# Making phi(q) of the first part for four head pairs at once, and one denominator for two score tiles

## The chip, the cores and the metric

The kernel runs on one core of a Trainium2 chip. Its time is the device time of one execution, in microseconds; smaller is better. The engines that matter here are PE (TensorE, the matmuls), ACT (ScalarE), DVE (VectorE), POOL (GpSimd) and SP, which issues the DMAs. They run side by side and wait for each other through semaphores.

## The reference, cut to what matters

An attention layer with a memory term feeds two feed-forward layers. B, H, S, D = 4, 8, 576, 64; 2304 tokens, width 512, hidden width 2048.

```python
scores = scale * q @ k.T, causal;  a = exp(scores - max)
a /= a.sum(-1) + 1e-09             # the denominator
local = a @ v
q_p = phi(q)                       # phi(x) = where(x > 0, x, exp(x) - 1) + 1
mem_out = (q_p @ M_prev) / (q_p @ z_prev + 1e-06)
g = 1 / (1 + exp(-beta))           # per head
attn = g * mem_out + (1 - g) * local
x = moe(attn)                      # x @ w_in, relu squared, s * . + b, @ w_out
out = moe2(x)                      # x @ w_in, a clipped square, @ w_out
```

## The kernel before, in words

The eight heads of a batch are four **head pairs** (two heads of 64 fill 128 partitions). The queries are cut into eight **parts**: for each of four batches first the tokens 0 to 255 (group `lo`, tiles 1 and 0), later the tokens 256 to 575 (group `hi`). The first two parts are computed ahead of everything; after them the blocks of the first feed-forward layer follow, with the other parts between them.

Nothing in the program is ordered by hand. Each operation is given to a planner (`Plan`, L108) with its engine, or several engines to choose from, and a cost; the planner lays out one order for each engine, and fixes on which engine an elementwise operation runs. So an edit at one place can move instructions at many others. Where the planner sees PE without work in the first phase it puts in idle matmuls on a tile of zeros (`zr`, L1379); they compute nothing that is used.

For one head pair of a `lo` part the work is:

- `att_front` (L769), **phi**: `qn + 1` on POOL (L801), exp(qn) on ACT (L522, the helper's line), min and max of both on DVE (L804), times z on DVE or POOL (L806, L805), a sum for each head on DVE (L807), two small DVE operations that make 1 / ((sum + 1e-6)(1 + exp(-beta))) (L808, L811), and phi times that on POOL or DVE (L812, L813). PE transposes the result (L820), and a copy takes it out of PSUM.
- `att_scores` (L830): PE makes the scores of tiles 1 and 0 (L861, eight matmuls). DVE adds the mask and takes the minimum of the negated scores (L877: 256 columns of tile 1 and 128 of tile 0 for each head). ACT takes exp with its sum (L522). DVE makes the **denominator** of each tile, `(sum + 1e-9) * (1 + exp(beta))`, in two small operations (L891, L894), and ACT, POOL or DVE multiplies the array by it (L903, L901, L902).
- `att_flip` (L907, transposes at L921, copies at L537 or L538) and `att_sum` (L928, matmuls at L937 and L948): transposes, then memory term and a @ v in one PSUM bank, whose result is split into a high and a low half for the feed-forward layer (`xx`, L537 and L529).

`constants` (L565) makes 1 + exp(beta) and 1 + exp(-beta) from the row that is loaded with z, and four DVE operations of 64 partitions (L573, L575) turn the first into the two orders that a joint tile of two heads needs.

In the same early time the weights of the first layer come in by DMA as 32 chunks of 64-bit words, and each is **converted** by two elementwise operations on ACT or POOL (L596 or L598, L602 or L600) and two on DVE (L605, L607), then split in two halves (L537 or L542, L529 or L533). The feed-forward matmuls of the first layer are L1008 to L1010 and L1071 to L1076.

In the trace the tiles of the first two parts lie in buffers that later hold weights, and have their names: `wor8` to `wor11` (phi, its helper, its transposed copy, q) and `wir12` to `wor15` (the score arrays).

Of the kernel before, what the change touches and what calls it, by code (L numbers as in the profile page):

```python
# [373 lines left out]
def tile_kernel(ctx: ExitStack, tc: tile.TileContext, qk_in, nv_in, z_in, w_in, w_out, w2_in, w2_out, out):  # L374
# [190 lines left out]
    def constants(zb):  # L565

        def row(a, e):
            return zb.t[:, H * D + a:H * D + e]
        act(lambda: con[:, 16:24], lambda: row(0, 8), AF.Exp, 8, [zb], ["con"], ATT)
        act(lambda: con[:, 24:32], lambda: row(0, 8), AF.Exp, 8, [zb], ["con"], ATT, scale=-1.0)  # L570
        dve(0.08, lambda: nc.vector.tensor_scalar(con[:, 16:32], con[:, 16:32], 1.0, None, ALU.add), ["con"], ["con"], ATT)
        for j in range(2):
            dve(0.08, lambda rows=slice(64 * j, 64 * j + 64), j=j: nc.vector.tensor_scalar(  # L573
                con[rows, 32:36], con[rows, 16:24].rearrange("p (n two) -> p n two", two=2)[:, :, j], 1.0, None, ALU.mult), ["con"], ["con"], ATT)
            dve(0.08, lambda rows=slice(64 * j, 64 * j + 64), j=j: nc.vector.tensor_scalar(  # L575
                con[rows, 36:40], con[rows, 16:24].rearrange("p (n two) -> p n two", two=2)[:, :, 1 - j], 1.0, None, ALU.mult), ["con"], ["con"], ATT)
        dve(0.08, lambda: nc.vector.tensor_scalar(con[:, 0:2], row(8, 10), 1.0, None, ALU.mult), [zb], ["sb"], W1)
        dve(0.05, lambda: nc.vector.memset(con[:, 4:5], 0.5), [], ["sb"], W1)
        dve(0.05, lambda: nc.vector.memset(con[:, 5:6], 1.0), [], ["sb"], W1)
# [186 lines left out]
    def load_z(b, zb):  # L766
        dma(lambda: zb.t, lambda: z_in[b], P * (H * D + 16) * 4, [], [zb], LOAD if first_qk[2:] else ATT, [zb], None if first_qk[2:] else "first")

    def att_front(hp, g, qn, q_key, zb):  # L769

        nt, nq = len(GROUPS[g]), GLEN[g]
        t0, n2 = min(GROUPS[g]), nt * P
        ee, xt, pg = (x.take() for x in ((E_EE, E_UZ, E_PG) if early_part[0] else (R_EE, R_UZ, R_PG)))
        cf = R_CF.take()
        hs = slice(hp * P, hp * P + P)

        def e():
            return ee.t[:, 0:n2]

        def pz():  # L780
            return xt.t[:, 0:n2]

        def c():
            return cf.t[:, 0:2 * nt]

        def cells(x):
            return x.t[:, 0:n2].rearrange("p (t d) -> p t d", d=D)
# [4 lines left out]
        def zz():
            return zb.t[:, hs].unsqueeze(1).broadcast_to([P, nt, P])

        def cc():
            return c().unsqueeze(2).broadcast_to([P, 2 * nt, D])

        def c2():
            return c().rearrange("p (t h) -> p t h", h=2)

        add([("POOL", c_pool(n2), lambda: nc.gpsimd.tensor_scalar(pz(), qn(), 1.0, 1.0, ALU.add, ALU.mult)),  # L801
             ("DVE", c_dve(n2, "cp"), lambda: nc.vector.tensor_scalar(pz(), qn(), 1.0, None, ALU.add))], [q_key], [xt], ATT, [xt])
        act(e, qn, AF.Exp, n2, [q_key], [ee], ATT, acq=[ee])
        dve(c_dve(n2), lambda: nc.vector.scalar_tensor_tensor(e(), e(), 1.0, pz(), ALU.min, ALU.max), [xt], [ee], ATT)  # L804
        add([("POOL", c_pool(n2, "tt"), lambda: nc.gpsimd.tensor_tensor(tiles3(xt), tiles3(ee), zz(), ALU.mult)),  # L805
             ("DVE", c_dve(n2), lambda: nc.vector.tensor_tensor(tiles3(xt), tiles3(ee), zz(), ALU.mult))], [ee, zb], [xt], ATT)  # L806
        dve(c_dve(n2), alone(lambda: nc.vector.tensor_reduce(c(), cells(xt), AX.X, ALU.add)), [xt], [cf], ATT, [cf])  # L807
        dve(0.08, lambda: nc.vector.scalar_tensor_tensor(  # L808
            c2(), c2(), 1e-6, con[:, 24 + 2 * hp:26 + 2 * hp].unsqueeze(1).broadcast_to([P, nt, 2]), ALU.add, ALU.mult),
            ["con"], [cf], ATT)  # L810
        dve(0.09, alone(lambda: nc.vector.reciprocal(c(), c())), [], [cf], ATT)  # L811
        add([("POOL", c_pool(n2, "tt") - 0.13, lambda: nc.gpsimd.tensor_tensor(cells(ee), cells(ee), cc(), ALU.mult)),  # L812
             ("DVE", c_dve(n2), lambda: nc.vector.tensor_tensor(cells(ee), cells(ee), cc(), ALU.mult))], [cf], [ee], ATT)  # L813
# [16 lines left out]
    def att_scores(g, items, mems=()):  # L830
# [38 lines left out]
        for hp, qk, t, c0, c1, places in items:  # L869
# [3 lines left out]
            pi = 0 if c0 == 0 else 1  # L873

            m0 = 0 if c1 < w else 640 if t == 4 else 512 - t * P + c0
            for j, (a, (x, at)) in enumerate(zip(arrays, places)):
                dve(c_dve(c1 - c0) + 0.02, alone(lambda a=a, s=s, z=zs[x], c0=c0, c1=c1, m0=m0, pi=pi, j=j, at=at, ao=ao: nc.vector.tensor_tensor_reduce(  # L877
                    a.t[:, ao + c0:ao + c1], z.t[:, at:at + c1 - c0], mask[:, m0:m0 + c1 - c0], -SCALE,
                    BIG if pi == 0 else s.t[:, j:j + 1], ALU.add, ALU.min, s.t[:, 2 * pi + j:2 * pi + j + 1])),
                    [zs[x], "mask", "zero_aa", (a, "new"), (s, "new")], [(a, hp, t), (s, "min", j)], ATT)  # L880
            if c1 < w:
                continue
            for j, a in enumerate(arrays):
                def view(w=w, a=a, ao=ao):
                    return a.t[:, ao:ao + w]

                act(view, view, AF.Exp, w, [(s, "min", j)], [(a, hp, t), (s, "sum", j)],
                    ATT, ap=2, bias=lambda s=s, x=2 * pi + j: s.t[:, x:x + 1], scale=-1.0,
                    accum_out=lambda s=s, x=4 + j: s.t[:, x:x + 1])
            c = 32 + hp + 4 * turned(hp, t) if t == 4 else 16 + 2 * hp  # L890
            dve(0.13, lambda s=s, nh=nh, c=c: nc.vector.scalar_tensor_tensor(  # L891
                s.t[:, 6:6 + nh], s.t[:, 4:4 + nh], 1e-9, con[:, c:c + nh], ALU.add, ALU.mult),
                [(s, "sum", j) for j in range(nh)] + ["con"], [(s, "r")], ATT)
            dve(0.08, alone(lambda s=s, nh=nh: nc.vector.reciprocal(s.t[:, 8:8 + nh], s.t[:, 6:6 + nh])), [(s, "r")], [(s, "i")], ATT)  # L894
            for j, a in enumerate(arrays):
                def view(w=w, a=a, ao=ao):
                    return a.t[:, ao:ao + w]

                def col(s=s, j=j):
                    return s.t[:, 8 + j:9 + j]  # L900
                add([("POOL", c_pool(w) + 0.09, lambda view=view, col=col: nc.gpsimd.tensor_scalar(view(), view(), col(), 1.0, ALU.mult, ALU.mult)),  # L901
                     ("DVE", c_dve(w, "cp") + 0.06, lambda view=view, col=col: nc.vector.tensor_scalar(view(), view(), col(), None, ALU.mult)),  # L902
                     ("ACT", c_act(w, 1), lambda view=view, col=col: nc.scalar.activation(view(), view(), AF.Copy, scale=col()))],  # L903
                    [(s, "i")], [(a, hp, t)], ATT)
# [554 lines left out]
```

## Time and profile before

| | us |
|---|---|
| median of 3 runs (973.88 to 974.11) | 973.88 |
| the profiled execution | 974.04 |
| its span, first to last instruction | 972.2 |
| PE busy | 963.5 (99%) |
| DVE busy | 660.0 (68%) |
| ACT busy | 582.0 (60%) |
| POOL busy | 225.4 (23%) |

The span is 1.84 us shorter than the profiled execution's own time. The granted TensorE clock is at full speed in every slice. The shares are means over stages: busy shares of the first 100 us are far from these. PE's busy time also holds the idle matmuls, so a busy PE is not always a PE that does needed work.

### The profile page before, as it was taken

To read this page: it belongs to the slowest core of one execution; us is meant where nothing else is said; L and a number is where in the kernel's file an instruction comes from. 1 tells how busy PE (TensorE), PEld (TensorE's weight loads), DVE (VectorE), ACT (ScalarE), POOL (GpSimd) and SP (SyncE) were. 2 spreads that over 40 slices of the span, in tenths; PEclk is the share of its full clock that TensorE was granted. 3 is DMA by queue.
4 is the path that set the end of the run, shared out by engine and by line. 5 is a ranking of instruction groups with operands and counts; after the bars stand their busy time and mean duration, and the time that the engine had idled before them with its cause. 6 is when DMAs were issued, how large, how long until landed. Compare 5 with 4: busy or idle time off the path is not lost.

```text
span 972.2 us, 19818 instructions
## 1 busy us (share of the span) xinstructions
PE 963.5 (99%) x7548; PEld 870.8 (90%) x7548; DVE 660.0 (68%) x1548; ACT 582.0 (60%) x1340; POOL 225.4 (23%) x339
## 2 busy tenths in 40 slices
PE   9999999999999999999999999999999999999998
PEld 7799999999999989999998888989998899998897
DVE  7899754655555556546599976887989447676652
ACT  7999866755556556555656666655666234354323
POOL 6501221311122113112212412333233111121100
PEclk9999999999999999999999999999999999999999
DMA  9690023222212212212044434535346952230310
GB/s 352 223 410 8 23 88 99 71 64 77 69 51 72 65 57 89 63 45 91 2 133 139 151 130 168 190 107 208 125 157 228 376 187 77 65 110 11 109 36 31
DMA packets 51136, 115.64 MB, mean 119 GB/s; under 512 B 5217, under 2 KB 16993, under 8 KB 51041
## 3 DMA queue, kind: packets, MB, share of 16 engines
q1 hardware_dynamic: 51040, 114.38, 34.6%
q8 instruction: 59, 0.97, 0.4%
q14 instruction: 37, 0.29, 0.1%
HBM read 87.62 MB, written 26.74 MB: 118 GB/s over the span
## 4 chain that ended last, share of the span: by engine, by line
PE 93%; ACT 4%; issue 1%; DVE 1%; POOL 0%; DVEq 0%; ACTq 0%; POOLq 0%
PE hb L1008 7%; PE hb L1009 6%; PE hb L1010 6%; PE yb L1076 6%; PE yb L1071 5%; PE yb L1072 5%; PE ab L861 5%; PE ab L948 5%; PE ab L921 4%; PE yb L1281 3%; PE yb L1282 3%; PE yb L1288 3%; PE ab L1281 3%; PE ab L1282 3%; PE ab L1288 3%; PE ab L1248 3%
## 5 line engine op out<-in xcount | busy, mean ns | idle before, releaser
L1008 PE MATMUL hb<-xx,wi 128*128 128x256 f32 (+1 forms) x512 | 152.3, 297 | 0.1
L1009 PE MATMUL hb<-xx,wi 128*128 128x256 f32 (+1 forms) x512 | 149.5, 292 | 0.0
L1010 PE MATMUL hb<-xx,wi 128*128 128x256 f32 (+1 forms) x512 | 149.5, 292 | 0.0
L1071 PE MATMUL yb<-gg,wo 128*128 128x256 f32 (+1 forms) x394 | 103.5, 293 | 0.8 <-ACT gg L537 0.4
L1008 PEld LDWEIGHTS hb<-xx,wi 128*128 128x128 f32 x512 | 96.4, 188 | 4.6 <-issue 0.7
L1010 PEld LDWEIGHTS hb<-xx,wi 128*128 128x128 f32 x512 | 96.2, 188 | 2.9
L1009 PEld LDWEIGHTS hb<-xx,wi 128*128 128x128 f32 x512 | 96.2, 188 | 2.8
L1072 PE MATMUL yb<-gg,wo 128*128 128x256 f32 (+1 forms) x394 | 98.7, 281 | 0.0
L522 ACT ACTIVATE aa<-aa,sm 128x512 f32<-128x512 f32 (+4 forms) x112 | 69.7, 626 | 24.5 <-DVE sm L877 24.5
L877 DVE CUSTOM_DVE_ANT_0 aa<-ab,mask 128x512 f32<-128x512 f32 (+3 forms) x112 | 56.4, 553 | 40.8 <-PE ab L861 40.8
L1071 PEld LDWEIGHTS yb<-gg,wo 128*128 128x128 f32 x394 | 74.2, 188 | 3.6 <-issue 0.9
L529 DVE TENSOR_TENSOR gg<-rr,gg 128x256 fp32r<-128x256 f32 (+1 forms) x105 | 46.1, 442 | 44.4 <-ACT gg L537 32.9
L1072 PEld LDWEIGHTS yb<-gg,wo 128*128 128x128 f32 x394 | 74.3, 189 | 0.5
L1076 PE MATMUL yb<-gg,wo 128*128 128x256 f32 (+1 forms) x394 | 73.2, 295 | 0.0
L1052 ACT ACTIVATE rr<-hb 128x256 f32<-128x256 f32 (+1 forms) x96 | 40.6, 422 | 48.3 <-PE hb L1010 48.0
L542 POOL TENSOR_SCALAR gg<-rr 128x256 fp32r<-128x256 f32 x58 | 27.9, 481 | 140.1 <-ACT rr L1056 61.9
L1076 PEld LDWEIGHTS yb<-gg,wo 128*128 128x128 f32 x394 | 55.4, 188 | 2.5 <-issue 1.0
L1248 PE MATMUL ab<-xx,wi 128*128 128x256 f32 (+1 forms) x203 | 54.5, 274 | 0.0
L1250 PE MATMUL ab<-xx,wi 128*128 128x256 f32 x196 | 54.5, 278 | 0.0
L1251 PE MATMUL ab<-xx,wi 128*128 128x256 f32 x196 | 54.1, 276 | 0.0
L1248 PE MATMUL hb<-xx,wi 128*128 128x256 f32 (+1 forms) x194 | 52.2, 274 | 0.0
L1250 PE MATMUL hb<-xx,wi 128*128 128x256 f32 x188 | 52.2, 278 | 0.0
(348 smaller groups left out, 2850.6 us busy)
## 6 DMA issues: line engine op xcount, KB each, us to landing
w2d<-st SPq DMA_DIRECT2D x48, 256.0 KB, 3.4
nv<-in_nv_dram SPq DMA_DIRECT2D x16, 576.0 KB, 3.7
wir<-in_moe_w_in_dram SPq DMA_DIRECT2D x16, 512.0 KB, 9.7
wor<-in_moe_w_out_dram SPq DMA_DIRECT2D x16, 512.0 KB, 10.0
raw<-in_moe_w_in_dram SPq DMA_DIRECT2D x16, 512.0 KB, 3.9
raw<-in_moe_w_out_dram SPq DMA_DIRECT2D x16, 512.0 KB, 4.5
qk<-in_qk_dram SPq DMA_DIRECT2D x16, 448.0 KB, 3.3
wo<-w2d SPq DMA_DIRECT2D x12, 512.0 KB, 5.6
```

The lines of the kernel that those rows point to most:

```text
L522: nc.scalar.activation(o(), i(), func, **{a: b() if callable(b) else b for a, b in kw.items()})
L1008: nc.tensor.matmul(o, w_in_part(fi, 0)[:, kt, :], x_h(kt), start=kt == 0, stop=False)
L1009: nc.tensor.matmul(o, w_in_part(fi, 0)[:, kt, :], x_l(kt), start=False, stop=False)
L1010: nc.tensor.matmul(o, w_in_part(fi, 1)[:, kt, :], x_h(kt), start=False, stop=kt == NK - 1)
L1071: nc.tensor.matmul(yv(c), w_out_part(fi, 0)[:, cs], gg.t[0], start=fi == 0 and c % k == 0, stop=False)
L1072: nc.tensor.matmul(yv(c), w_out_part(fi, 1)[:, cs], gg.t[0], start=False, stop=False)
L1076: pe(c_mm(n), lambda c=c, cs=cs, gg=gg, fi=fi: nc.tensor.matmul(yv(c), w_out_part(fi, 0)[:, cs], gg.t[1], start=False, stop=fi == NF - 1 a ...
L1248: nc.tensor.matmul(o[:, c0:c1], sw(q, k, 0, kt), xo(k, 0, kt)[:, c0:c1], start=j == 0 and kt == 0 and c0 == 0, stop=False)
L1250: nc.tensor.matmul(o, sw(q, k, 0, kt), xo(k, 1, kt), start=False, stop=False)
L1281: nc.tensor.matmul(y.t, gh.t[:, cs], wo2(q, i, 0), start=first and jj == 0, stop=False)
L1282: nc.tensor.matmul(y.t, gh.t[:, cs], wo2(q, i, 1), start=False, stop=False)
L1288: pe(c_mm(512), widened(lambda q=q, y=y, cs=cs, jj=jj: nc.tensor.matmul(y.t, gl.t[:, cs], wo2(q, i, 0), start=False, stop=last and jj == 1 ...
```

## The change

Three edits:

1. In the first part alone (batch 0, `lo`) phi is made for all four pairs by single operations of 1024 columns (`att_phi` with four pairs); every other part calls the same function with one pair, as before. The 16 sums lie in a tile of their own (`cf_t`), and the 1 + exp(-beta) that they need comes repeated from `con[:, 32:48]`.
2. In `lo` parts the denominators of tiles 1 and 0 are made together, by one pair of small operations after the exps of both tiles, where each tile had its own pair.
3. The host lays beta into the z row in three orders (and repeated), so that the four operations of 64 partitions are gone. The row grows from 528 to 560 columns.

```diff
-        act(lambda: con[:, 16:24], lambda: row(0, 8), AF.Exp, 8, [zb], ["con"], ATT)
-        act(lambda: con[:, 24:32], lambda: row(0, 8), AF.Exp, 8, [zb], ["con"], ATT, scale=-1.0)
-        dve(0.08, lambda: nc.vector.tensor_scalar(con[:, 16:32], con[:, 16:32], 1.0, None, ALU.add), ["con"], ["con"], ATT)
-        for j in range(2):
-            dve(0.08, lambda rows=slice(64 * j, 64 * j + 64), j=j: nc.vector.tensor_scalar(
...
+        act(lambda: con[:, 16:32], lambda: row(0, 16), AF.Exp, 16, [zb], ["con"], ATT)
+        act(lambda: con[:, 32:48], lambda: row(16, 32), AF.Exp, 16, [zb], ["con"], ATT, scale=-1.0)
+        dve(0.08, lambda: nc.vector.tensor_scalar(con[:, 16:48], con[:, 16:48], 1.0, None, ALU.add), ["con"], ["con"], ATT)
...
+    def att_phi(hps, g, ees, xts, cf, cfs, qn, q_key, zb):
+
+        nh, nt = len(hps), len(GROUPS[g])
+        n2 = nh * nt * P
...
+        add([("POOL", c_pool(n2), lambda: nc.gpsimd.tensor_scalar(pz(), qn(), 1.0, 1.0, ALU.add, ALU.mult)),
...
+        act(e, qn, AF.Exp, n2, [q_key], ees, ATT, acq=ees)
+        dve(c_dve(n2), lambda: nc.vector.scalar_tensor_tensor(e(), e(), 1.0, pz(), ALU.min, ALU.max), xts, ees, ATT)
+        add([("POOL", c_pool(n2, "tt"), lambda: nc.gpsimd.tensor_tensor(tiles4(pz), tiles4(e), zz(), ALU.mult)),
...
+        dve(c_dve(n2), alone(lambda: nc.vector.tensor_reduce(c(), cells(pz), AX.X, ALU.add)), xts, [cf], ATT, own)
+        dve(0.08, lambda: nc.vector.scalar_tensor_tensor(c2(), c2(), 1e-6, gate(), ALU.add, ALU.mult), ["con"], [cf], ATT)
+        dve(0.09, alone(lambda: nc.vector.reciprocal(c(), c())), [], [cf], ATT)
...
+        if q_key == "first q":
+            if not hp:
+                first_ee.extend(E_EE.take() for _ in range(NP))
+                att_phi(range(NP), g, first_ee, [E_UZ.take() for _ in range(NP)], "first cf", lambda: cf_t, lambda: first_q, q_key, zb)
+            ee = first_ee[hp]
...
+            if t == 1:
+                continue
+            ts = (1, 0) if t == 0 else (t,)
...
+            dve(0.13, lambda part=part, k=k, nh=nh, c=c, n=len(ts): nc.vector.scalar_tensor_tensor(
+                part(4 + k), part(4), 1e-9, con[:, c:c + nh].unsqueeze(1).broadcast_to([P, n, nh]), ALU.add, ALU.mult),
```

The planner turns this into other orders. In DVE's order, soon after the scores of the second pair, where `wor8` is phi, `wor9` its helper and `wir14`, `wir15` the score arrays of the second pair, stood

```order
L877 ISA wir15_78,sm02_178<-ab3_116,mask_106 128x256
L877 ISA sm02_178 128x1
L804 SCALAR_TENSOR_TENSOR wor8_87<-wor8_87,wor9_88 128x256 x2
L571 TENSOR_SCALAR con_104<-con_104 128x16
L806 TENSOR_TENSOR wor9_88<-wor8_87,zb00_163 128x256
L573 TENSOR_SCALAR con_104<-con_104 64x4
L877 ISA wir14_77,sm03_179<-ab2_115,mask_106 128x128
L877 ISA sm03_179 128x1
L877 ISA wir15_78,sm03_179<-ab3_116,mask_106 128x128
```

and now stands

```order
L896 ISA wir14_77,sm01_177<-ab2_115,mask_106 128x256
L896 ISA sm01_177 128x1
L803 SCALAR_TENSOR_TENSOR wor8_87<-wor8_87,wor9_88 128x1024
L896 ISA wir14_77,sm01_177<-ab2_115,mask_106 128x128
L896 ISA sm01_177 128x1
L805 TENSOR_TENSOR wor9_88<-wor8_87,zb00_163 128x1024
L571 TENSOR_SCALAR con_104<-con_104 128x32
L896 ISA wor13_92,sm02_178<-ab1_114,mask_106 128x256
L896 ISA sm02_178 128x1
L806 TENSOR_REDUCE after_x_101<-wor9_88 128x16
L916 SCALAR_TENSOR_TENSOR sm00_176<-sm00_176,con_104 128x4
L807 SCALAR_TENSOR_TENSOR after_x_101<-after_x_101,con_104 128x16
```

Three operations of 1024 columns (the reduction has 16 results) have come between the mask operations of the second and third pair.

On PE, from the scores of the third pair (`wir9`) on, stood

```order
L861 MATMUL ab1_114<-wir9_72 128x128
L1379 MATMUL hb0_109<-zr_103 128x128
L861 MATMUL ab2_115<-wir9_72 128x256
L861 MATMUL ab3_116<-wir9_72 128x256
L861 MATMUL ab2_115<-wir9_72 128x128
L861 MATMUL ab3_116<-wir9_72 128x128
L1379 MATMUL hb0_109<-zr_103 128x128 x6
L921 MATMUL ab1_114<-ident_102,wir12_75 128x128 x2
```

and now stands

```order
L878 MATMUL ab1_114<-wir9_72 128x128
L1406 MATMUL hb0_109<-zr_103 128x128 x13
L878 MATMUL ab2_115<-wir9_72 128x256
L878 MATMUL ab1_114<-wir9_72 128x256
L878 MATMUL ab2_115<-wir9_72 128x128
L878 MATMUL ab1_114<-wir9_72 128x128
L948 MATMUL ab0_113<-ident_102,wir12_75 128x128
```

The fourth pair's scores now stand behind 13 idle matmuls instead of one, and take the bank `ab1` in place of `ab3`.

On ACT, up to the copy of the last transposes of the second part (`av01`, for its last pair), stood

```order
L537 ACTIVATE at01_185<-ab2_115 128x512
L537 ACTIVATE wi2_732<-stg0_95 128x512
L596 ACTIVATE stg1_96<-wor2_81 128x512
L537 ACTIVATE wor10_89<-ab1_114 128x256
L537 ACTIVATE av01_188<-ab0_113 128x256
```

and now stands

```order
L597 ACTIVATE wir3_66<-wir3_66 128x512
L591 ACTIVATE stg1_96<-wor2_81 128x512
L591 ACTIVATE stg2_97<-wir3_66 128x512
L537 ACTIVATE wi2_692<-stg0_95 128x512
L537 ACTIVATE at01_185<-ab3_116 128x512
L537 ACTIVATE wor10_89<-ab1_114 128x256
L537 ACTIVATE av01_188<-ab0_113 128x256
```

Two conversions of a later weight chunk (`wir3`) have come ahead of these copies.

## Rows read from the trace of the kernel before

**Rows 1.** Page, part 1: busy time of each engine, share of the span, instructions.

```profile
PE 963.5 (99%) x7548; PEld 870.8 (90%) x7548; DVE 660.0 (68%) x1548; ACT 582.0 (60%) x1340; POOL 225.4 (23%) x339
```

**Rows 2.** Busy time by stretch: stretch, length; busy PE, PEld, DVE, ACT, POOL; clock; DMA share, GB/s.

```profile
6.30:17.00 10.70, 9.68 (x76) 7.72 (x74) 10.49 (x59) 9.95 (x39) 6.52 (x12) 1.00 1.05 391
17.00:30.00 13.00, 13.00 (x115) 10.43 (x113) 12.26 (x58) 13.00 (x46) 11.44 (x19) 1.00 0.99 385
30.00:47.00 17.00, 15.94 (x143) 12.73 (x140) 15.06 (x62) 17.00 (x56) 9.55 (x13) 1.00 0.49 162
47.00:54.00 7.00, 6.57 (x60) 6.19 (x57) 6.77 (x13) 7.00 (x17) 0.00 (x0) 1.00 1.02 410
54.00:100.00 46.00, 45.28 (x384) 44.45 (x383) 43.23 (x84) 46.00 (x113) 5.87 (x10) 1.00 0.43 172
100.00:500.00 400.00, 400.00 (x3920) 369.22 (x3919) 230.14 (x718) 247.99 (x656) 83.70 (x150) 1.00 0.21 66
```

**Rows 3.** The same stretches, busy time of the idle matmuls (L1379) alone.

```profile
6.30:17.00 10.70, 3.70 (x26) 3.13 (x26) 1.00 1.05 391
17.00:30.00 13.00, 1.44 (x10) 1.27 (x10) 1.00 0.99 385
30.00:47.00 17.00, 1.82 (x12) 1.58 (x12) 1.00 0.49 162
```

**Rows 4.** Timeline of the first part: start, time taken, engine, line.

```profile
6.29 0.72 ACT L522 ACTIVATE wor<-wor 128x256 f32<-128x256 f32 x2 [4.28 <-DMA wor<-in_nv_dram]
...
7.52 0.42 DVE L877 CUSTOM_DVE_ANT_0 wir<-ab,mask 128x256 f32<-128x256 f32 x1
...
8.21 0.76 DVE L804 SCALAR_TENSOR_TENSOR wor<-wor,wor 128x256 f32<-128x256 f32 x2
...
9.05 0.91 POOL L805 TENSOR_TENSOR wor<-wor,zb 128x256 f32<-128x256 f32 x1 [1.19 <-DVE con L571]
...
9.29 0.69 DVE L573 TENSOR_SCALAR con<-con 64x4 f32<-64x4 f32 x1
...
10.24 1.13 PE L861 MATMUL ab<-wir 64*128 64x256 f32 x8 [0.46 <-DVE sm L877]
...
12.21 0.15 DVE L891 SCALAR_TENSOR_TENSOR sm<-sm,con 128x2 f32<-128x2 f32 x1
...
12.29 0.23 DVE L808 SCALAR_TENSOR_TENSOR cf<-cf,con 128x4 f32<-128x4 f32 x2
...
15.00 1.11 PE L861 MATMUL ab<-wir 64*128 64x256 f32 x8
...
16.04 0.70 PE L937 MATMUL ab<-wor,wir 128*128 128x256 f32 x2
```

**Rows 5.** Instructions of L804 and L812: duration min/median/max in ns, first and last start.

```profile
L804 DVE SCALAR_TENSOR_TENSOR wor<-wor,wor x8: 405/418/805, 8.2 to 40.0; 128x256 f32<-128x256 f32 x8
...
L812 POOL TENSOR_TENSOR wor<-wor,cf x8: 614/615/968, 13.2 to 42.5; 128x256 f32<-128x256 f32 x8
```

**Rows 6.** Chain that ended last, 20 to 60 us: start, time that the step holds.

```profile
25.15 0.80 ACT wor L903 x2
...
27.43 0.60 DVE stg L605
...
33.92 0.29 ACT wir L903
...
46.10 0.27 ACT av L537
46.37 0.52 ACT wo L537
...
58.08 1.10 ACT stg L596 x2
```

**Rows 7.** PE's timeline at the last sum of the second part, and the wait after it.

```profile
44.96 0.83 PE L1379 MATMUL hb<-zr 128*128 128x128 f32 x6
46.16 0.70 PE L937 MATMUL ab<-wor,wor 128*128 128x256 f32 x2 [0.37 <-ACT wor L537]
```

More of the change, by code (lines that the diff above doesn't have):

```diff
@@ L418, in tile_kernel @@
     xl = [xx[:, (NK + i) * XC:(NK + i + 1) * XC] for i in range(NK)]
-    t32([P, 16], "after_x")
+    cf_t = t32([P, 16], "after_x")
     ident = t32([P, P], "ident")
     zr = t32r([P, P], "zr")
-    con = t32([P, 40], "con")
+    con = t32([P, 48], "con")
     cs_t = t32([P, NK], "cs")
@@ L568, in row @@
             return zb.t[:, H * D + a:H * D + e]
-        act(lambda: con[:, 16:24], lambda: row(0, 8), AF.Exp, 8, [zb], ["con"], ATT)
-        act(lambda: con[:, 24:32], lambda: row(0, 8), AF.Exp, 8, [zb], ["con"], ATT, scale=-1.0)
-        dve(0.08, lambda: nc.vector.tensor_scalar(con[:, 16:32], con[:, 16:32], 1.0, None, ALU.add), ["con"], ["con"], ATT)
-        for j in range(2):
-            dve(0.08, lambda rows=slice(64 * j, 64 * j + 64), j=j: nc.vector.tensor_scalar(
[L574 to L577, printed above, removed]
+        act(lambda: con[:, 16:32], lambda: row(0, 16), AF.Exp, 16, [zb], ["con"], ATT)
+        act(lambda: con[:, 32:48], lambda: row(16, 32), AF.Exp, 16, [zb], ["con"], ATT, scale=-1.0)
+        dve(0.08, lambda: nc.vector.tensor_scalar(con[:, 16:48], con[:, 16:48], 1.0, None, ALU.add), ["con"], ["con"], ATT)
+        dve(0.08, lambda: nc.vector.tensor_scalar(con[:, 0:2], row(32, 34), 1.0, None, ALU.mult), [zb], ["sb"], W1)
         dve(0.05, lambda: nc.vector.memset(con[:, 4:5], 0.5), [], ["sb"], W1)
@@ L769, in att_front @@
+    first_ee = []
     def att_front(hp, g, qn, q_key, zb):
@@ L772, in att_front @@
         t0, n2 = min(GROUPS[g]), nt * P
[L773 to L787, printed above, removed]
+        if q_key == "first q":
[3 more added lines that the diff above has]
+            ee = first_ee[hp]
+        else:
+            ee, xt = (x.take() for x in ((E_EE, E_UZ) if early_part[0] else (R_EE, R_UZ)))
+            cf = R_CF.take()
+            att_phi([hp], g, [ee], [xt], cf, lambda: cf.t, qn, q_key, zb)
@@ L789, in tiles3 @@
+        pg = (E_PG if early_part[0] else R_PG).take()
         def tiles3(x):
             return x.t[:, 0:n2].rearrange("p (t n) -> p t n", n=P)
[L792 to L813, printed above, removed]
@@ L837, in att_scores @@
             if t == 0:
-                att_open[hp, 0] = (att_open[hp, 1][0], R_SM.take(), 256)
-                new.append(att_open[hp, 0][1])
+                att_open[hp, 0] = (*att_open[hp, 1][:2], 256)
             elif c0 == 0:
@@ L872, in att_scores @@
             nh = len(arrays)
-            pi = 0 if c0 == 0 else 1
+            pi = int(c0 > 0)
+            low = 2 * (pi or t == 0)
+            tot = 6 if t == 0 else 4
             m0 = 0 if c1 < w else 640 if t == 4 else 512 - t * P + c0
             for j, (a, (x, at)) in enumerate(zip(arrays, places)):
-                dve(c_dve(c1 - c0) + 0.02, alone(lambda a=a, s=s, z=zs[x], c0=c0, c1=c1, m0=m0, pi=pi, j=j, at=at, ao=ao: nc.vector.tensor_tensor_reduce(
+                dve(c_dve(c1 - c0) + 0.02, alone(lambda a=a, s=s, z=zs[x], c0=c0, c1=c1, m0=m0, pi=pi, j=j, at=at, ao=ao, low=low: nc.vector.tensor_tensor_reduce(
                     a.t[:, ao + c0:ao + c1], z.t[:, at:at + c1 - c0], mask[:, m0:m0 + c1 - c0], -SCALE,
-                    BIG if pi == 0 else s.t[:, j:j + 1], ALU.add, ALU.min, s.t[:, 2 * pi + j:2 * pi + j + 1])),
-                    [zs[x], "mask", "zero_aa", (a, "new"), (s, "new")], [(a, hp, t), (s, "min", j)], ATT)
+                    BIG if pi == 0 else s.t[:, j:j + 1], ALU.add, ALU.min, s.t[:, low + j:low + j + 1])),
+                    [zs[x], "mask", "zero_aa", (a, "new"), (s, "new")], [(a, hp, t), (s, "min", t, j)], ATT)
             if c1 < w:
@@ L885, in view @@
                     return a.t[:, ao:ao + w]
[L887 to L904, printed above, removed]
+                act(view, view, AF.Exp, w, [(s, "min", t, j)], [(a, hp, t), (s, "sum", t, j)],
+                    ATT, ap=2, bias=lambda s=s, x=low + j: s.t[:, x:x + 1], scale=-1.0,
+                    accum_out=lambda s=s, x=tot + j: s.t[:, x:x + 1])
@@ new lines, in att_scores, with part @@
+            if t == 1:
+                continue
+            ts = (1, 0) if t == 0 else (t,)
+            c, k = 24 + hp + 4 * turned(hp, t) if t == 4 else 16 + 2 * hp, nh * len(ts)
+            def part(x, s=s, k=k, n=len(ts)):
+                return s.t[:, x:x + k].rearrange("p (t h) -> p t h", t=n)
+            dve(0.13, lambda part=part, k=k, nh=nh, c=c, n=len(ts): nc.vector.scalar_tensor_tensor(
+                part(4 + k), part(4), 1e-9, con[:, c:c + nh].unsqueeze(1).broadcast_to([P, n, nh]), ALU.add, ALU.mult),
+                [(s, "sum", x, j) for x in ts for j in range(nh)] + ["con"], [(s, "r")], ATT)
@@ new lines, in att_scores, with view, col @@
+            dve(0.08, alone(lambda s=s, k=k: nc.vector.reciprocal(s.t[:, 4 + 2 * k:4 + 3 * k], s.t[:, 4 + k:4 + 2 * k])), [(s, "r")], [(s, "i")], ATT)
+            for n, x in enumerate(ts):
+                w, ao = x * P + rows_of(x), att_open[hp, x][2]
+                for j, a in enumerate(arrays):
+                    def view(w=w, a=a, ao=ao):
+                        return a.t[:, ao:ao + w]
+                    def col(s=s, x=4 + 2 * k + nh * n + j):
+                        return s.t[:, x:x + 1]
+                    add([("POOL", c_pool(w) + 0.09, lambda view=view, col=col: nc.gpsimd.tensor_scalar(view(), view(), col(), 1.0, ALU.mult, ALU.mult)),
+                         ("DVE", c_dve(w, "cp") + 0.06, lambda view=view, col=col: nc.vector.tensor_scalar(view(), view(), col(), None, ALU.mult)),
+                         ("ACT", c_act(w, 1), lambda view=view, col=col: nc.scalar.activation(view(), view(), AF.Copy, scale=col()))],
+                        [(s, "i")], [(a, hp, x)], ATT)
@@ L1417, in _laid @@
     z = _np.asarray(inputs["z_prev"]).reshape(B, H * D)
-    row = _np.zeros((B, H * D + 16), z.dtype)
-    row[:, 0:H * D] = z
-    for at, x in ((0, "beta"), (8, "moe_s"), (9, "moe_b")):
+    rows = _np.zeros((B, P, H * D + 48), z.dtype)
+    rows[:, :, 0:H * D] = z[:, None]
+    for at, x in ((0, "beta"), (32, "moe_s"), (33, "moe_b")):
         x = _np.asarray(inputs[x]).reshape(-1)
-        row[:, H * D + at:H * D + at + x.size] = x
-    laid["z"] = _np.broadcast_to(row[:, None], (B, P, H * D + 16))
+        rows[:, :, H * D + at:H * D + at + x.size] = x
+    beta = _np.asarray(inputs["beta"]).reshape(NP, 2)
+    for j in range(2):
+        rows[:, 64 * j:64 * j + 64, H * D + 8:H * D + 12] = beta[:, j]
+        rows[:, 64 * j:64 * j + 64, H * D + 12:H * D + 16] = beta[:, 1 - j]
+    rows[:, :, H * D + 16:H * D + 32] = _np.broadcast_to(beta[:, None], (NP, 2, 2)).reshape(-1)
+    laid["z"] = rows
     laid["qk"] = _np.concatenate([qt[..., 0:256], down(k), qt[..., 256:]], axis=-1)
```

29 lines of the change are left out of this document (27 added, 2 removed).

## The prediction

> **What bounds the kernel now.** I read the page's busy times first, then busy time by stretch, then the same table for the idle matmuls alone, and then the timeline of the first 17 us. PE is busy for 99% of the span [rows 1], so what counts is needed PE work plus the time in which PE has none. From 100 to 500 us PE is busy in all 400 us while VectorE is busy for 230 and ScalarE for 248 [rows 2]: there nothing that those two save can reach the end. Before 100 us it is different. PE's own idle time plus the idle matmuls is 1.02 + 3.70 us from 6.3 to 17, 0 + 1.44 from 17 to 30, 1.06 + 1.82 from 30 to 47, then 0.43 up to 54 and 0.72 up to 100 [rows 2, 3]. That is 9.0 us up to 47 and 1.2 behind it, and it is all that this change can play for (PE's time ahead of 6.3 us is the first loads' and stays). The change adds and removes no needed matmul, so a microsecond of PE idle time won or lost here arrives at the end.
>
> Who makes PE wait there? ScalarE is busy for all of 17 to 47 us, VectorE for 12.26 of 13 and then 15.06 of 17, GpSimd for 11.44 of 13 and then 9.55 of 17 [rows 2]. ScalarE is the bound, VectorE close behind.
>
> The orders of before and after meet at one point, where I do the sum: the last `att_sum` of the second part, 46.16 us in the trace, held up by a ScalarE copy [rows 7]. Ahead of it PE has the same needed matmuls in both orders, only 24 idle ones after the first eight become 27. So the whole effect up to there is how much earlier or later this sum starts.
>
> **The change, part by part.**
>
> *Joint phi.* The rows price 256 columns on VectorE at 0.34 us of the queue (two in 0.76, the last 0.42 long) [rows 4], and 512 columns at 0.60 [rows 6]: about 1.02 ns a column, so 1024 columns hold VectorE for some 1.13 us (between 1.13 and, if stretched as the longest L804 was, 0.805 against 0.418 [rows 5], 2.2; I take 1.13, since 0.418 is the median). Four of these replace ten of 0.34, and two small operations replace eight, which follow each other after 0.08 us [rows 4]: 4.7 us in place of 4.0, because two z products that GpSimd made, at 0.91 [rows 4], and four last products, at 0.615 [rows 5], now lie on VectorE. GpSimd loses about 4.3 us, VectorE gains 0.7.
>
> What is queued behind: I walked VectorE's new order with these prices. The second pair's first mask operation begins at 7.52 [rows 4] and ends at 7.87; min-max to 9.0; a mask operation; z product to 10.35; the third pair's first mask operation to 10.8; reduction to 11.9; small operations and mask operations to 12.8. Only then has bank `ab1` come free, and the fourth pair's scores start near 13.0 where they started at 10.24 [rows 4]. 13 idle matmuls fill the hole. But little waits for those scores. The first transposes need the first denominators, about 12.6 us as before, and the first `att_sum` needs phi's last product (ending near 14.8), a transpose and a copy: near 16.4 instead of 16.04 [rows 4]. By then PE had also done one set of scores of the second part (1.11 us from 15.00 [rows 4]); it now has one more phi transpose instead, two short matmuls. PE is some 0.9 us behind at 17 us. After that phi is finished for all four pairs, where before two were still to come. Walking on, the second sum starts level (near 20), the third earlier, the fourth about level in work done.
>
> *Joint denominators.* In each `lo` part eight pairs of small operations become four: up to the common point fifteen of 0.08 us [rows 4] go, 1.2 us of VectorE. It adds a wait: tile 1's multiplication now waits for the exps of tile 0, two of 0.29 plus their sums, under 0.8 us. Behind it on PE stand tile 1's transposes; the new order puts tile 0's first and other pairs' scores between, so I cost it at nothing in the second part; in the first it lies inside the 16.4 above. In the third and fourth `lo` part both gain and wait lie beside a PE that is never idle [rows 2]: nothing.
>
> *Beta in three orders.* Four VectorE operations go; one took 0.69 us at 9.29 [rows 4], with three short ones about 0.9 us of VectorE. The load of z grows by 16 KB in 264, ahead of the third pair's q and k: 0.04 us at 391 GB/s [rows 2], which lies under the mask operations that those scores wait for anyway.
>
> *VectorE together:* +0.7 - 1.2 - 0.9 = -1.4 us up to the common point, and the planner fills that again with four copies of about 0.34 and one conversion of 0.60, 2.0 us. So VectorE has 0.6 us more than before, and 2.7 us of idle time between 17 and 47 to hold it [rows 2].
>
> *ScalarE up to the common point.* Counted in the orders: four exps of 256 columns (0.36 each [rows 4]) become one of 1024 (about 1.05): -0.4. Five copies of 256 columns fewer at 0.27, three multiplications of 128 at 0.29, two of 256 at 0.40, one relu at 0.27; one copy of 512 more at 0.52, three conversions more at 0.55 [rows 6]: -1.35 - 0.87 - 0.80 - 0.27 + 0.52 + 1.65. Sum -1.5 us. Against it stands more waiting early: ScalarE idles 0.75 us from 6.3 to 17 [rows 2]; in my walk the third pair's exps wait for VectorE until 12.5, and I count 1.45 us. So the common point comes 1.5 - 0.7 = **0.8 us earlier**.
>
> *Behind it.* Three conversions, 1.65 us of ScalarE, are already done. From 47 to 100 us ScalarE is the busy engine again and PE idles 1.15 us [rows 2]; I take a third of it, -0.4. Far behind, in the second layer, the new order has one idle matmul where there was none: the planner sees a hole there, +0.2.
>
> **The sum:** 974.04 - 0.8 - 0.4 + 0.2 = 973.0 us for the profiled execution, whose span is 1.84 below its time; the median is 0.16 below the profiled execution: **972.9 us**. What a measurement can tell from no change is about 0.2%, 1.95 us: under 971.9 is faster, over 975.8 slower.
>
> **The rivals.**
>
> *A. GpSimd's relief counts in full.* GpSimd is busy for 88% of 17 to 30 us [rows 2] and loses 4.3 us. If the three engines share their work evenly, 5.8 us (its 4.3 and ScalarE's 1.5) make 1.9 us on each; with the conversions that are ahead, and with half of the 4.3 us of PE idle time between 17 and 47 gone [rows 2, 3], the kernel gains 2 to 4: 971. For it: all three are nearly full. Against it: ScalarE, which holds PE, gains only 1.5.
>
> *B. The long operations stretch: slower.* The longest L804 took 0.805 us in place of 0.418, and an L812 0.968 in place of 0.615 [rows 5]; each had work of the other engine beside it. If the four operations of 1024 columns hold VectorE for 2.2 us instead of 1.13, the first part ends 4.2 us later than in my walk, of which PE can make up about the 1.7 us that the forecast still finds: +2.5, 976.4. It decides from a stretch of about 1.7 on all four. Against it: in the new order GpSimd's first product is done before them, and it waits for a weight load next; seven of eight L804 were not stretched so far that the median moved.
>
> [...]
>
> *C. It is all refilled.* The planner spends what is freed on conversions, the copy that PE waits for still ends a full ScalarE queue, and the early 0.9 us is just made up: 973.9 ± 0.7.
>
> **How the numbers follow.** Forecast 0.5 (972.0 to 974.2 by its own bounds), A 0.2, C 0.2, B 0.1. A lies under 971.9 for most of its weight, the forecast for little: faster 0.22. B gives slower 0.09, some unseen stall of a new order behind 100 us 0.02: slower 0.11. Same 0.67. The range takes A's middle and the near side of B: 970.9 to 975.9.
>
> **What would show it.** Right: the fourth pair's scores near 13 us; PE's idle time plus idle matmuls up to 17 us larger by about 1 us, smaller behind it by nearly 2; the last sum of the second part near 45.4 us; long VectorE operations of 1.2 us. B: those at 2 us, that sum behind 47 us. A: that sum before 44 us. C: at 46. Wrong in another way: PE idle between 100 and 500 us, or the TensorE clock, now full in every stretch [rows 2], lower behind the longer hole.

## The result, and where the time went

The changed kernel takes 986.31 us (986.02 to 986.81, 4 runs), the kernel before, beside it, 973.88 us: a ratio of 1.0129, 95% interval 1.0117 to 1.0142. It is 12.4 us slower, outside the range of 970.9 to 975.9. The profiled execution took 986.47 us with a span of 984.7. Its page, part 1, against [rows 1]:

```profile
PE 978.3 (99%) x7556; PEld 883.1 (90%) x7556; DVE 655.4 (67%) x1502; ACT 584.9 (59%) x1340; POOL 212.8 (22%) x325
```

PE is busy for 14.8 us more, with eight matmul records more (the idle ones, two records each). ScalarE is busy for 2.9 us more, VectorE for 4.6 and GpSimd for 12.6 us less. The stretches of [rows 2], of the kernel after (stretch, length; busy PE, PEld, DVE, ACT, POOL; clock; DMA share, GB/s):

```profile
6.30:17.00 10.70, 10.04 (x83) 8.45 (x81) 10.67 (x48) 9.64 (x35) 3.81 (x7) 1.00 1.05 393
17.00:30.00 13.00, 12.74 (x117) 9.86 (x113) 9.94 (x41) 12.81 (x48) 10.85 (x19) 1.00 1.01 389
30.00:47.00 17.00, 16.88 (x143) 13.10 (x141) 16.40 (x62) 16.89 (x50) 9.06 (x13) 1.00 0.53 179
47.00:54.00 7.00, 7.00 (x61) 6.85 (x58) 6.80 (x14) 7.00 (x17) 0.45 (x1) 1.00 1.02 413
54.00:100.00 46.00, 45.94 (x381) 44.98 (x380) 43.40 (x83) 46.00 (x114) 9.60 (x14) 1.00 0.42 165
100.00:500.00 400.00, 400.00 (x3886) 369.52 (x3885) 223.20 (x695) 246.11 (x650) 79.73 (x143) 1.00 0.21 64
```

And the idle matmuls (L1406 now) alone, against [rows 3]:

```profile
6.30:17.00 10.70, 5.16 (x40) 4.69 (x40) 1.00 1.05 393
17.00:30.00 13.00, 1.01 (x6) 0.91 (x6) 1.00 1.01 389
30.00:47.00 17.00, 1.20 (x10) 0.97 (x8) 1.00 0.53 179
```

Up to 100 us the change did about what was forecast: PE's idle time plus idle matmuls, 10.19 us before, is 1.10 + 7.37 = 8.47, so 1.7 us less where the forecast had 1.2. The timeline of PE has the fourth pair's scores at 12.49, the first sum at 15.99 and the last sum of the second part at 45.67, where [rows 4, 7] have 10.24, 16.04 and 46.16:

```profile
12.49 1.09 PE L878 MATMUL ab<-wir 64*128 64x256 f32 x8
15.99 0.70 PE L964 MATMUL ab<-wor,wir 128*128 128x256 f32 x2
45.67 0.70 PE L964 MATMUL ab<-wor,wor 128*128 128x256 f32 x2
```

The loss is in the last row of the stretches. From 100 to 500 us PE is busy throughout in both kernels at a granted clock of 1.00, but in the same 400 us it gets through 3886 matmuls where it got through 3920 [rows 2]. Nothing waits there: the matmuls themselves are slower. One line each of before and after in the second layer (L1251 is L1278 after) shows it; the columns are the duration's minimum, median and maximum in ns, and the first and last start in us:

```profile
L1251 PE MATMUL ab<-xx,wi x196: 276/276/279, 610.7 to 934.2; 128*128 128x256 f32 x196
```

```profile
L1278 PE MATMUL ab<-xx,wi x196: 276/281/282, 614.7 to 946.1; 128*128 128x256 f32 x196
```

The same 196 matmuls of the same shape take 281 ns instead of 276. From start to start (they overlap) the 256-column matmuls of `xx` in the second layer take 113.4 ns in the mean before and 117.6 after. For 512 columns there are two levels too: the matmuls that read `g2` take 226.9 ns before and 233.1 after. I call them the **fast** and the **slow pace**. Counting an interval below 115.5 ns as fast, 99% of the 256-column `xx` matmuls of the second layer are fast before, 5% after; in the first layer the two paces alternate, 75% fast before, 36% after.

To weigh this, each fp32r matmul's time from start to start is compared with 113.4 ns (256 columns) or 226.9 (512), and what lies above is summed; intervals more than 13 ns above are waits and left out. This **excess** is 6.4 us before and 21.2 after: +14.8, and 2.4 less for all the rest makes the 12.4 us.

### The profile page after: what moved, and what is told of

Read it like the earlier page. It is cut to its first block, busy times and chain, and to the rows that moved or that the text cites. A ratio compares the mean times of both kernels' runs of the same rounds, so it can differ in the third digit from the quotient of the medians.

```text
span 984.7 us, 19747 instructions
## 1 busy us (share of the span) xinstructions
PE 978.3 (99%) x7556; PEld 883.1 (90%) x7556; DVE 655.4 (67%) x1502; ACT 584.9 (59%) x1340; POOL 212.8 (22%) x325
## 4 chain that ended last, share of the span: by engine, by line
PE 93%; ACT 3%; DMA 2%; issue 0%; DVE 0%; POOL 0%; SPq 0%; DVEq 0%; ACTq 0%
PE hb L1035 7%; PE hb L1036 6%; PE hb L1037 6%; PE yb L1103 6%; PE yb L1098 5%; PE yb L1099 5%; PE ab L975 4%; PE ab L878 4%; PE ab L948 4%; PE ab L1308 3%; PE yb L1315 3%; PE ab L1309 3%; PE ab L1315 3%; PE yb L1308 3%; PE yb L1309 3%; PE ab L1275 3%
## 5 line engine op out<-in xcount | busy, mean ns | idle before, releaser
L1098 PE MATMUL yb<-gg,wo 128*128 128x256 f32 (+1 forms) x394 | 104.9, 295 | 0.0
L1099 PE MATMUL yb<-gg,wo 128*128 128x256 f32 (+1 forms) x394 | 100.2, 283 | 0.0
L1099 PEld LDWEIGHTS yb<-gg,wo 128*128 128x128 f32 x394 | 74.2, 188 | 0.5
L1103 PE MATMUL yb<-gg,wo 128*128 128x256 f32 (+1 forms) x394 | 73.8, 296 | 0.0
L1079 ACT ACTIVATE rr<-hb 128x256 f32<-128x256 f32 (+1 forms) x94 | 37.6, 400 | 44.2 <-PE hb L1037 43.8
L542 POOL TENSOR_SCALAR gg<-rr 128x256 fp32r<-128x256 f32 x54 | 25.3, 469 | 141.0 <-ACT rr L1083 69.3
L1278 PE MATMUL ab<-xx,wi 128*128 128x256 f32 x196 | 55.0, 281 | 0.0
```

What stands on the lines that cost most here:

```text
L1098: nc.tensor.matmul(yv(c), w_out_part(fi, 0)[:, cs], gg.t[0], start=fi == 0 and c % k == 0, stop=False)
L1099: nc.tensor.matmul(yv(c), w_out_part(fi, 1)[:, cs], gg.t[0], start=False, stop=False)
L1103: pe(c_mm(n), lambda c=c, cs=cs, gg=gg, fi=fi: nc.tensor.matmul(yv(c), w_out_part(fi, 0)[:, cs], gg.t[1], start=False, stop=fi == NF - 1 a ...
```

## What the experiments showed

What in the change can slow down matmuls that it doesn't touch? The diff has two candidates. **Theory A, the address:** `con` grew from 40 to 48 columns, so every tile allocated behind it lies 32 bytes further in each partition: `rr`, `gg`, `xp`, `xr`, `g2` and the attention tiles; weights (`wi`, `wo`) and `xx` lie ahead of it and did not move. (The tile `zb` grew by 128 bytes as well, which moves the attention tiles behind it by that much more; no run below takes this back in the changed kernel.) **Theory B, the stream:** the new order of instructions puts PE into the slow pace by itself.

All times below stand beside runs of the kernel before on the same chip (973.5 to 973.8 us).

**The change with the later tiles that the feed-forward layers read at their old addresses.** This is the **first kernel** of what follows.

```diff
-    t32([P, 48], "before_x")
+    con = t32([P, 48], "before_x")
-    con = t32([P, 48], "con")
+    t32([P, 40], "con")
```

> The changed kernel with the small table `con` (48 columns) laid where the spacer `before_x` (48 columns) lies, and an empty tile of 40 columns left in `con`'s old place: every tile behind it that the matmuls read or that conversions write (gg, xp, xr, g2, qk, nv) has the address that it had before the change; instructions and their order are those of the changed kernel. Theory A (address): the loss is a slower matmul pace that comes from the 32 bytes by which `con` grew; the time falls to 971 to 973.5 us, the median interval of 256-column matmuls from 118 to 113.5 ns, and the gain of about 1.5 us that the early stretches of the trace show is all that is left of the change. Theory B (stream): the pace comes from the new order of instructions, whatever the addresses; 985 to 987 us.

Measured: 972.22 us (ratio 0.9985, 0.9976 to 0.9995). The 14 us are gone, with the changed order and the larger `zb`. Theory B falls, and `zb` is not the cause. The same line is fast again:

```profile
L1278 PE MATMUL ab<-xx,wi x196: 276/276/279, 608.4 to 931.8; 128*128 128x256 f32 x196
```

**The kernel before with only the 32 bytes.**

```diff
-    con = t32([P, 40], "con")
+    con = t32([P, 48], "con")
```

> The kernel before, with `con` widened from 40 to 48 columns and nothing else: the order is as before, the tiles behind `con` lie 32 bytes further. Theory A (address): 985 to 988 us, 256-column matmuls at 118 ns, early stretches as before. Theory B (stream): 973.5 to 974.5 us.

Measured: 986.73 us (1.0132, 1.0115 to 1.0149), with the order of before. The whole loss comes from eight columns that nothing reads:

```profile
L1251 PE MATMUL ab<-xx,wi x196: 276/281/282, 615.1 to 946.9; 128*128 128x256 f32 x196
```

**64 bytes instead of 32.** In the changed kernel:

```diff
-    con = t32([P, 48], "con")
+    con = t32([P, 56], "con")
```

> The changed kernel with `con` at 56 columns, 8 of them unused, so that the tiles behind it lie 64 bytes further than before the change where the change put them 32 further. Theory A with a period of 64 bytes: 971 to 974 us. Theory A with a longer period (128, 256 or 512 bytes, which the spacers in the kernel would also fit): slow or half slow, 976 to 988 us. Theory B: 985 to 987 us.

Measured: 981.05 us (1.0076, 1.0060 to 1.0091). So 64 bytes also cost 7.4 us. But the slow matmuls are fewer: those that read `g2` (512 columns, 389 ns before) are slow at 393, those of `xx` mostly fast, with a median of 276. Both rows are of this kernel:

```profile
L1309 PE MATMUL yb<-wo,g x64: 393/393/393, 636.5 to 947.5; 128*128 128x512 f32 x64
```

```profile
L1278 PE MATMUL ab<-xx,wi x196: 276/276/286, 613.0 to 940.3; 128*128 128x256 f32 x196
```

**Which tiles.** The first kernel with a gap behind `gg`, so that only the tiles of the phases are off:

```diff
     gg_t = t32r([P, 6 * T], "gg")
+    t32([P, 8], "after_gg")
```

> As the first run here (the changed kernel with `con` in the spacer), but with a spacer of 8 columns behind `gg`: gg, rr and mask stay at the addresses of before, the tiles of the phases (qk, nv, xp, xr, g2) lie 32 bytes further. Theory A with xp and g2 at its root (moving operands that every block of layer 1 and the second half of layer 2 read): 980 to 987 us. Theory A with gg alone at its root: 971 to 974 us. Theory B: 985 to 987 us.

Measured: 983.01 us (1.0094, 1.0079 to 1.0109). The phases' tiles carry most of it. The second layer is slow, `xx` included, though neither `xx` nor its weights moved:

```profile
L1279 PE MATMUL ab<-xx,wi x196: 281/281/282, 611.3 to 942.9; 128*128 128x256 f32 x196
```

**Is it the address or a distance?** The kernel before with everything moved by 32 bytes, weights and `xx` too:

```diff
+    t32([P, 8], "first")
     raws = {nm: [sb.tile([P, 2 * DM], U32, name=f"{nm}r{i}", tag=f"{nm}{i}") for i in range(NF)] for nm in ("wi", "wo")}
```

> The kernel before with an empty tile of 8 columns ahead of all tiles: weights, xx, gg, xp and g2 all lie 32 bytes further, so that every distance between two of them is that of the kernel before; the order is as before. Theory A1 (what counts is the distance between the moving operand and the weights of the same stretch of matmuls): 973 to 975 us, 256-column matmuls at 113.5 ns as before. Theory A2 (what counts is each address by itself, a multiple of 64 bytes being fast): 985 to 990 us, slower even than with 32 bytes behind con, since xx and the weights are off as well.

Measured: 973.59 us (0.9999, 0.9990 to 1.0008), and the line is fast:

```profile
L1252 PE MATMUL ab<-xx,wi x196: 276/276/279, 610.7 to 934.1; 128*128 128x256 f32 x196
```

So addresses 32 bytes further are not bad by themselves: with all tiles moved the time is 973.59 us, with only those behind `con` moved it is 986.73. The loss came with tiles that moved against others.

**256 bytes.** In the kernel before:

```diff
-    con = t32([P, 40], "con")
+    con = t32([P, 104], "con")
```

> The kernel before with con at 104 columns: everything behind con lies 256 bytes further, weights and xx stay. Period of 256 bytes or less (64 is out by the third run: 64 bytes cost 7.4 us): 973 to 975 us. A period of 512 bytes or more: 977 to 987 us.

Measured: 973.80 us (1.0000, 0.9990 to 1.0009). 256 bytes change nothing; 32 bytes, in the same kernel, cost 13.1 us, and 64, in the changed kernel, 7.4.

**Other places for one tile.** The first kernel with `gg` alone moved, by 128 bytes as shown, and by 192 bytes with 48 and 16 columns in place of 32 and 32:

```diff
+    t32([P, 32], "before_gg")
     gg_t = t32r([P, 6 * T], "gg")
+    t32([P, 32], "after_gg")
```

> The first kernel of this study (the change, with con in the spacer) with gg alone moved by 128 bytes, 32 empty columns ahead of it and 32 behind; the tiles of the phases move by 256, which the sixth run showed to cost nothing. The distance of gg as moving operand from its weights wo becomes 320 bytes, 64 modulo 256, where it was 192. If 192 is the one good distance for 256-column matmuls (0 and 224 were slow): those of gg in layer 1, 1150 of them at a mean of 115.2 ns, go to 118 ns, and the matmuls between them may be drawn along: 975 to 978 us. If 64 is a good distance as well: 970 to 972.5.

> The same with gg moved by 192 bytes (48 empty columns ahead, 16 behind): distance 384 bytes, 128 modulo 256. By the one good distance: 975 to 978 us; if 128 is good as well: 970 to 972.5 us, with the gg matmuls of layer 1 nearer to 113.4 ns than the 115.2 of the first kernel.

Measured: 978.20 us (1.0046, 1.0031 to 1.0061) and 978.19 us (1.0047, 1.0030 to 1.0064). Both places of `gg` cost 6.0 us against the 972.22 us of the first kernel. (The distances that the two expectations name are worked out from the sizes of the tiles in the source; no view shows an address.) L1099 of the first kernel, the same line with 128 bytes (L1101 there), and the line ahead of it with 192 (L1100; these two lines have the same median of 277 before), with medians of 276, 280 and 282 ns (both widths are in one row here):

```profile
L1099 PE MATMUL yb<-gg,wo x394: 276/276/394, 33.6 to 583.9; 128*128 128x256 f32 x192, 128*128 128x512 f32 x5
```

```profile
L1101 PE MATMUL yb<-gg,wo x394: 275/280/397, 34.6 to 589.0; 128*128 128x256 f32 x192, 128*128 128x512 f32 x5
```

```profile
L1100 PE MATMUL yb<-gg,wo x394: 274/282/398, 34.1 to 588.4; 128*128 128x256 f32 x192, 128*128 128x512 f32 x5
```

Put together, the median durations in ns of three groups: `xx` of the second layer (the line of the first pair of rows above, writing `ab`), `gg` of the first layer (the rows above, both widths), and the matmuls that read `g2` (512 columns, writing `yb`; `g2` holds the weights and `wo` moves). A dash stands for a value that no view here shows; "mean" marks a mean.

| kernel | what has moved | time, us | `xx` | `gg` | `g2` |
|---|---|---|---|---|---|
| before | nothing | 973.88 | 276 | 277 | 389 |
| before | all tiles, by 32 bytes | 973.59 | 276 | – | 389 (mean) |
| before | behind `con`, by 256 | 973.80 | 276 | – | 389 (mean) |
| before | behind `con`, by 32 | 986.73 | 281 | – | 394 (mean) |
| after | behind `con`, by 32 | 986.31 | 281 | 280 | 395 |
| after | behind `con`, by 64 | 981.05 | 276 | 282 | 393 |
| first kernel | nothing of the three | 972.22 | 276 | 276 | – |
| first kernel | the phases' tiles, by 32 | 983.01 | 281 | 276 | 395 |
| first kernel | `gg` by 128, the phases' tiles by 256 | 978.20 | – | 280 | – |
| first kernel | `gg` by 192, the phases' tiles by 256 | 978.19 | – | 282 | – |

From start to start, where the neighbours have the same width, `gg` of the first layer takes 115.5 ns before and 118.1 after for 256 columns: 56% of these matmuls are fast before, 5% after. In the second layer `gg` takes 113.4 before and 118.5 after. Not every matmul of the kernel before has the fast pace: `xx` with 512 columns in the first layer takes 233.3 ns before and 232.7 after. Each run moved a tile against all others at once, so which two tiles have to lie well to one another is not shown.

**Does a slow matmul slow its neighbours?** In the kernel before, `g2` alone moved by 32 bytes:

```diff
-    TILES[1]["before_g2"] = ([P, 16], F32)
+    TILES[1]["before_g2"] = ([P, 24], F32)
```

> The kernel before with g2 alone 32 bytes further (its spacer before_g2 at 24 columns in place of 16); order and all other addresses as before. g2 is read in the second half only. If each matmul has the pace of its own addresses, only those that read g2 slow down: 412 of 512 columns by 6.2 ns and 107 by 5, 3.1 us: 976.7 us. If the slow step also holds for the matmuls that follow, whose addresses have not moved: xx against wi (1111, 113.4 to 117.8 ns) and gg against wo (184) as well, another 5.7 us: 982 to 983 us.

Measured: 983.30 us (1.0095, 1.0077 to 1.0114). Both rows are of this kernel. The matmuls that read `g2` (here 512 columns, 389 ns before) are slow at 395, and so are those that read `xx`, at unmoved addresses, at 281:

```profile
L1282 PE MATMUL yb<-wo,g x64: 392/395/395, 635.2 to 950.6; 128*128 128x512 f32 x64
```

```profile
L1251 PE MATMUL ab<-xx,wi x196: 276/281/282, 611.4 to 943.4; 128*128 128x256 f32 x196
```

The 188 matmuls of the same line that write `hb` (622.7 to 942.0 us) take 281 ns at the minimum, the median and the maximum, where they have a median of 276 before; from start to start 99% of the 1111 `xx` matmuls of the second layer were fast there. So moving `g2` slowed matmuls that do not read it, and that is why 32 bytes at a few tiles cost 12 us: of the 14.8 us of excess that the change added, 7.1 lie in the 256-column matmuls of `xx`, which had not moved. It does not always go that way: in the 64-byte run, with `g2` (393 ns) and `gg` (282) slow as well, `xx` has a median of 276; and `wo` by `wo` (512 columns) keeps its median of 389 here, beside the slow `xx`. Both paces occur at the same addresses: in the kernel after, all 54 fast `xx` matmuls of the second layer follow each other in one stretch (646.0 to 652.0 us), and the stretches around it are slow.

**The change repaired with one number.**

```diff
-    con = t32([P, 48], "con")
+    con = t32([P, 104], "con")
```

> The changed kernel with con at 104 columns, 56 of them unused, so that what lies behind it is 256 bytes further than before the change in place of 32. By the period of 256 bytes this repairs the change in one number: 971.5 to 973 us, as the first run. If the first run was fast for another reason (con in the spacer): 981 to 987.

Measured: 972.67 us (0.9986, 0.9976 to 0.9996), the same as the first kernel (972.22) within what can be told. The two beat the kernel before by 1.2 and 1.4 us.

**The two halves of the change, at the old addresses.** Joint denominators without joint phi, then joint phi without joint denominators:

```diff
-        if q_key == "first q":
+        if False:
             if not hp:
```

> The changed kernel at the addresses of before (con in the spacer), with phi made pair by pair as before: joint denominators and beta's orders alone. The recorded prediction has most of the early gain from the denominators (15 small VectorE operations) and beta (4): 972.4 to 973.2 us, the last sum of the second part between 45.3 and 45.8 us. If joint phi carries the gain: 973.4 to 974.0, that sum at 46.

```diff
-                att_open[hp, 0] = (*att_open[hp, 1][:2], 256)
+                att_open[hp, 0] = (att_open[hp, 1][0], R_SM.take(), 256)
...
```

The rest of that diff makes each tile's denominator as before.

> The changed kernel at the addresses of before, with the denominators made tile by tile as before: joint phi and beta's orders alone. The recorded prediction has VectorE 0.7 us fuller by joint phi and 0.9 us freer by beta, ScalarE 0.4 us freer, GpSimd 4.3 us freer: 973.0 to 973.8 us, idle matmuls up to 17 us near 5.2 us against 3.70. If GpSimd's relief is what counts (rival A): 972.0 to 972.6, as with both parts.

Measured: 972.40 us (0.9990, 0.9981 to 0.9999) and 972.71 us (0.9989, 0.9980 to 0.9998), the second 0.3 us under what the recorded working gave it. (The 11 times of the first spread from 971.83 to 973.58.) Each half alone gives about what both give together; the gains don't add. Two marks missed: the last sum of the second part, expected between 45.3 and 45.8 with the denominators alone, lies at 43.04 (44.11 with phi alone), and the idle matmuls up to 17 us with phi alone take 5.77 us where 5.2 was expected. That sum can't be compared with 46.16 either: it has 24 and 30 records of feed-forward matmuls ahead of it, where the kernel before has 36. The excess tells more (profiled executions, us):

| kernel | span | excess over the fast pace | the rest |
|---|---|---|---|
| before | 972.2 | 6.4 | 965.8 |
| before, all moved by 32 | 972.1 | 6.1 | 966.0 |
| before, 256 behind `con` | 972.1 | 5.7 | 966.4 |
| after | 984.7 | 21.2 | 963.5 |
| after, old addresses | 969.9 | 5.8 | 964.1 |
| after, 256 behind `con` | 970.9 | 4.6 | 966.3 |
| denominators only | 969.8 | 4.5 | 965.3 |
| phi only | 970.9 | 5.2 | 965.7 |
| before, 32 behind `con` | 985.4 | 20.6 | 964.8 |

The loss is all in the third column. The gain at the other addresses isn't cleanly in either: in the first layer the paces alternate (75% of `xx` fast before), and the excess of these seven kernels reaches from 4.5 to 6.4 us. With 256 bytes behind `con` the changed kernel's gain is in the excess alone, and the rest is 0.5 us longer than before.

## Why the prediction was wrong, point by point

**The step that failed** is the sentence "The change adds and removes no needed matmul, so a microsecond of PE idle time won or lost here arrives at the end." It priced the needed matmuls of both kernels alike. The count was right and the price was not: 14.8 us of excess came in with the 8 columns of `con` (14.2 with nothing but these columns, in the kernel before), a line of the diff that the prediction gave no cost at all. "Wrong in another way" named idle time of PE from 100 to 500 us and the TensorE clock. Neither moved: PE has none, and the clock is 1.00 in every stretch above. Busy time at full clock was taken for a constant.

**The rest of the forecast fits, in part by luck.** With the addresses restored the time is 972.22 and 972.67 us against a forecast of 972.9, and most marks of the first 100 us came. But it is not shown that these bring the gain: the excess, which the forecast knew nothing of, fell by 0.6 and 1.8 us in them. Nor did the sum's division hold: from it joint phi and beta alone were expected at 973.0 to 973.8 us, and they took 972.71, as little as all three parts with 256 bytes behind `con`. Point by point, from the trace after:

- The long VectorE operations: 1.22 us each, forecast 1.13 and "long VectorE operations of 1.2 us".

```profile
7.66 1.22 DVE L803 SCALAR_TENSOR_TENSOR wor<-wor,wor 128x1024 f32<-128x1024 f32 x1
9.00 1.22 DVE L805 TENSOR_TENSOR wor<-wor,zb 128x1024 f32<-128x1024 f32 x1
10.57 1.21 DVE L806 TENSOR_REDUCE after_x<-wor 128x16 f32<-128x1024 f32 x1
13.40 1.22 DVE L810 TENSOR_TENSOR wor<-wor,after_x 128x1024 f32<-128x1024 f32 x1
```

- So rival B did not come. (Its 976.4 counts the 4.2 us from the walk and adds 2.5 to the time before; added to the forecast it would be 975.4.) In the new order GpSimd works beside them for 0.42 us at the reduction (10.57 to 10.99) and 0.03 us at the last product, and not at all beside the other two. These rows therefore do not show what a long GpSimd operation beside them would cost.
- The fourth pair's scores: 12.49 us, forecast 13. The first sum: 15.99, forecast 16.4. PE's idle time plus idle matmuls up to 17 us: 4.72 before, 5.82 after, forecast about 1 more. Behind it up to 100 us: 5.47 before, 2.65 after, forecast nearly 2 less; the first kernel, where `xx` has its 276 ns again, has 2.74.
- The last sum of the second part: forecast 45.4. The two kernels with the change and the fast pace have the same order and show 44.99 and 45.95, so two kernels of one order lie a microsecond apart here. The forecast lies between, but 45.95 is all but rival C's mark of 46, so this mark does not decide between the two. First kernel, then 256 bytes behind `con`:

```profile
44.99 0.70 PE L964 MATMUL ab<-wor,wor 128*128 128x256 f32 x2
```

```profile
45.95 0.70 PE L964 MATMUL ab<-wor,wor 128*128 128x256 f32 x2
```

- The late idle matmul, +0.2: two records, 0.38 us, at 736.7 us.
- Rivals A (971) and C (973.9): the two repaired kernels' intervals, 0.9976 to 0.9996 of 973.7, reach from 971.4 to 973.3. Neither rival's middle lies in them, the forecast does; C's own range (from 973.2) just touches them.

**What stays open.** How much of the 1.2 to 1.4 us is PE's early idle time and how much another share of the fast pace in the first layer: in the profiled executions the excess fell by 0.6 in one repaired kernel and by 1.8 in the other. That the loss comes from how the tiles lie to one another is shown (973.59 us with all tiles 32 bytes further, 986.73 with only those behind `con`); which tiles have to lie how is not. What in the chip makes it, and why `xx`, unmoved, has a median of 281 ns with `g2` 32 bytes off but 276 in the 64-byte run, is open.

## What to carry to other kernels

A diff that resizes an on-chip tile can move all tiles behind it, as `con` did here (986.73 us with nothing but its 8 columns): compare the addresses before and after, and put the new columns where they move nothing, or pad by an amount that was measured to cost nothing (256 bytes here: 973.80 us in the kernel before, 972.67 in the changed one). Where PE is already 99% busy, read the duration of an untouched matmul line first: 5 ns on one line (276 to 281) told more here than all waits together. And an empty tile with a name like `before_x` in a tuned kernel may be there for an address: here 32 bytes more in `before_g2` cost 9.5 us.

## What the runs showed of the chip that was not expected

- Back-to-back fp32r matmuls of this kernel showed two paces at a granted clock of 1.00, from start to start: for 256 columns 113.4 ns before and 117.6 after (`xx`, second layer), for 512 columns 226.9 and 233.1 (those that read `g2`).
- The pace changed with the place of tiles, at the same instructions in the same order: with 8 empty columns behind `con` the kernel before took 986.73 us and its `xx` line 281 ns instead of 276; with all tiles 32 bytes further (973.59 us) or 256 bytes behind `con` (973.80) the line stayed at 276.
- Moving one tile slowed matmuls that do not read it: with `g2` alone 32 bytes off, the `xx` line went from 276 to 281 ns at unmoved addresses, and the kernel lost 9.5 us.
